# Weaving the output projection of the first attention segments into the last segment's q and k projections

## The chip, the cores and the metric

The kernel runs on one core of one Trainium2 chip. The metric is the device time of one execution in microseconds; the time given for a kernel is the median of its runs. A profiled execution shows the engines: TensorE (PE, with its weight loads as PEld), VectorE (DVE), ScalarE (ACT), GpSimd (POOL), and SyncE (SP), which issues nearly all DMAs.

## The reference

One transformer block on x of 2048 rows by 512 columns, with sa, ca, ga, sb, cb, gb the six modulation vectors of `silu(c) @ w_mod`:

```
h = layernorm(x) * (1 + ca) + sa
for s in 4 segments of 512 rows, 32 heads of 16:
    p     = softmax(q_s k_s^T / 4 + strictly-upper mask * -1e9)
    a_mem = phi(q_s) M / (phi(q_s) z + 1e-6)
    o_s   = g * a_mem + (1 - g) * (p v_s)        # g = sigmoid(beta), per head
    M, z += phi(k_s)^T v_s, sum of phi(k_s)
x = x + ga * (o @ wo)
h = layernorm(x) * (1 + cb) + sb
out = x + gb * (((h @ w_gate) * (h @ w_up)) @ w_down)
```

The mask puts −1e9 on the keys behind a query's own place (key index over query index). phi(t) is t + 1 above zero and exp(t) below.

## The kernel before, in words

All matrices that count are split into a high part and a remainder, and a product is three matmuls: high × high, remainder × high, high × remainder. A tile named `..H` is the high part (an ACT copy to a rounded type), `..L` the remainder (a subtraction on DVE or POOL).

There are two stages. The second is the gated network: for each of four segments, gate, up and down products (lines 1015 and 1036), with PE always busy. The first, in front of it, is one long loop over 32 units of four heads each (`NQ`), in which the attention of one unit is spread over several passes `v`, and everything else of the first stage is cut into small pieces and put between.

A pass has five slots. A slot emits, in this order: `q_step`, the scores of a later unit with queries in rows, on which DVE finds the maxima (two PSUM tiles, `lq0` and `lq1`, line 257); `flush()`, which emits DVE work put off in the list `later`; in slot 1 the products `tb` of the unit before (`av_step`); in slot 4 its transposes and division (`t_step`); `fill`, the pieces of other work; and `k_step`, the same scores transposed, with the exponent on ACT (line 296) and the causal select on POOL (line 299). PE's instructions keep the order in which they are written (`pe`), and so do DVE's inside the loop (`vec.eng = CV`); `pin` ties an instruction behind the last PE instruction written before it. A scheduler orders the rest by its own estimate.

`fill` takes pieces from two generators, `fa` first and then `fb`. Each yields a weight for the piece it has just emitted: 0.68 for three matmuls of 512 columns, 0.45 for four transposes. A slot with a share adds 0.25 × 5.5 to a credit, and pieces are emitted while the credit is above zero. A `yield False` ends the slot's filling at once and leaves the credit standing. `until` runs pieces without regard to credit where the next unit needs them. `weave(a, b, at)` runs generator `a` and advances `b` behind those weighted pieces of `a` whose numbers stand in `at`.

`fill_a` holds the q, k and v projections of the segments (`a_kq`, `a_v`), the first layer norm (`a_ln`), and the linear-attention memory (`a_mem`). `fill_b` holds what follows attention for segments 0 to 2: it closes the pool `pa` of the first generator and opens `bc` and `pb`; splits wo (`woH`, `woL`, line 776); loads the attention rows of a segment (`wo_load`, tiles `orl`), transposes them (`wo_op`, tiles `op`, with ACT writing `oH` at line 404 and DVE `oL`), multiplies by wo (`wo_row`, tiles `wops`, twelve matmuls for 128 rows), adds x (`wo_add`, tiles `xr`) and stores the sum; and it runs the second layer norm of segment 0 (`lnC`, transposes `ctp`, ACT `chf`) and the weight splits of the first two blocks of the gated network (`prep`). Segment 3 is done behind the loop.

PSUM tiles of all these pieces come from `bank`. Inside the loop `btag` is `["ms"]`, so there are two buffers for them.

Of the kernel before, what the change touches and what calls it, by code (L numbers as in the profile page):

```python
# [17 lines left out]
P = 128  # L18
S, D, H, DH, NSEG, L, F = 2048, 512, 32, 16, 4, 512, 1376
KT = D // P  # L20
NG = 4
# [36 lines left out]
def tile_kernel(ctx, tc, x, wq, wk_, wv, wo, beta, w_gate, w_up, w_down, c, w_mod, out):  # L58
# [82 lines left out]


    def ln(pool, hpool, xt, s, sc, sh, pfx, hb, fast):

# [33 lines left out]
        for d in range(KT):  # L178
            ps = bank(f"{pfx}tp{s}_{d}")
            for t in range(4):  # L180
                TP(ps[:, t * P:(t + 1) * P], xt[t][:, d * P:(d + 1) * P], ident)
            h = pool.tile([P, L], F32, tag="hf", name=f"{pfx}hf{s}_{d}", bufs=hb[2])
            A.activation(h, ps, AF.Identity, scale=sc[:, d:d + 1], bias=sh[:, d:d + 1])
            hi = hpool.tile([P, L], F32R, tag=hb[0].format(d), name=f"{pfx}hH{s}_{d}", bufs=hb[1])
            lo = hpool.tile([P, L], F32R, tag=hb[0].format(4 + d), name=f"{pfx}hL{s}_{d}", bufs=hb[1])
            if fast:
                V.tensor_copy(hi, h)
                V.tensor_sub(lo, h, hi.bitcast(F32))
            else:
                act.activation(hi, h, AF.Copy)  # L190
                nc.gpsimd.tensor_sub(lo, h, hi.bitcast(F32))
            hH.append(hi)
            hL.append(lo)
            yield 0.45
            if not first and d % 2 == 1:
                yield False
# [81 lines left out]
    def k_step(u, i):  # L278
# [113 lines left out]

    def wo_op(s, pb, rw, us, gs=range(NG)):

        for g in gs:
            op = bank(f"op{s}_{g}")
            for t in range(4):
                a = rw[t][:, g * P:(g + 1) * P]
                if s == NSEG - 1 and g == NG - 1:
                    a = orows[NSEG * NG - 1][:, t].rearrange("p h e -> p (h e)")  # L400
                TP(op[:, t * P:(t + 1) * P], a, ident)
            oH = pb.tile([P, L], F32R, tag="oH", name=f"oH{s}_{g}", bufs=6)
            oL = pb.tile([P, L], F32R, tag="oL", name=f"oL{s}_{g}", bufs=6)
            act.activation(oH, op, AF.Copy)
# [6 lines left out]
    def xr_load(s, pb):  # L411
        xrs = []
        for t in range(4):
            xr = pb.tile([P, D], F32, tag="xr", name=f"xr{s}_{t}", bufs=4)
            pin(nc.sync.dma_start(xr, x[rows(s, t), :]))
            xrs.append(xr)
        return xrs

    def wo_row(ps, t, us, gs):
        woH, woL = B["wo"]  # L420
        for i in gs:
            for j, (a, b) in enumerate(((us[i][0], woH), (us[i][1], woH), (us[i][0], woL))):
                MM(ps, a[:, t * P:(t + 1) * P], b[:, i, :], start=i == 0 and j == 0, stop=i == NG - 1 and j == 2)
            yield 0.68
# [4 lines left out]

    def wo_mm(s, us, pb):  # L430

        xrs = xr_load(s, pb)
        for t in range(4):
# [12 lines left out]


    papool, pa = open_pool(name="pa", bufs=2, reuse_waits="tile")
    nc.sync.dma_start(s_c, c)
# [132 lines left out]
    def load_g(nm, w, g):  # L582

        A, V = (CA if g == 0 else act), (CV if g == 0 and nm == "q" else nc.gpsimd)
        raw = staged(f"{nm}{g}")
        hi = wH[nm, g] = pa.tile([P, KT, P], F32R, name=f"w{nm}H{g}", bufs=1)
        lo = wL[nm, g] = pa.tile([P, KT, P], F32R, name=f"w{nm}L{g}", bufs=1)
        pin(nc.sync.dma_start(raw.rearrange("p (k c) -> p k c", c=P),
# [8 lines left out]
    def load_v():  # L597
        raws = []
        for k in range(KT):
            wH["v", k] = pa.tile([P, D], F32R, name=f"wvH{k}", bufs=1)  # L600
            wL["v", k] = pa.tile([P, D], F32R, name=f"wvL{k}", bufs=1)
            raws.append(staged(f"v{k}"))
# [161 lines left out]

    def wo_raw(k, pool, tag, n):
        raw = pool.tile([P, D], F32, tag=tag, name=f"wor{k}", bufs=n)
        pin(nc.sync.dma_start(raw, wo[k * P:(k + 1) * P, :]))
        nc.gpsimd.tensor_mul(raw, raw, gab)
        return raw

    def open_b():
        close(papool)
        B["bcpool"], B["bc"] = open_pool(name="bc", bufs=1, side="right", reuse_waits="tile")
        B["pbpool"], B["pb"] = open_pool(name="pb", bufs=2, reuse_waits="tile")
        pb = B["pb"]
        B["wo"] = woH, woL = [pb.tile([P, KT, D], F32R, name=n, bufs=1) for n in ("woH", "woL")]
        raws = B["raw"] + [wo_raw(k, pb, "x1", 4) for k in (2, 3)]
        yield
        for k in range(KT):
            pin(act.activation(woH[:, k, :], raws[k], AF.Copy))  # L780
            (vec if k % 2 else nc.gpsimd).tensor_sub(woL[:, k, :], raws[k], woH[:, k, :].bitcast(F32))
            yield

    def fill_a():
# [5 lines left out]
        for s in range(NSEG):  # L790
# [4 lines left out]
            for g in range(2 if s == 0 else 0, NG):  # L795
# [27 lines left out]
                if s > 0 and g == 0:  # L823
# [6 lines left out]
                    else:  # L830
                        yield from a_v(s)
                        B["orl"] = wo_load(0, wpool)
                        B["raw"] = [wo_raw(k, wpool, "wor", 2) for k in (0, 1)]
                if g == 1 and 0 < s < 3:
# [102 lines left out]
    for v in range(-2, NQ + 1):  # L937
        rate[0] = 5.5
        on, prev = 0 <= v < NQ, 0 <= v - 1 < NQ
        for slot in range(5):  # L940
# [14 lines left out]
            if v == NQ and slot == 2:  # L955
# [4 lines left out]
                us3 = []  # L960
                run(wo_op(3, B["pb"], o3, us3, range(NG - 1)))
            if prev and slot == 4:
# [19 lines left out]
    btag[:] = ["sm"]  # L982
    run(wo_op(3, B["pb"], o3, us3, (NG - 1,)))
    for t in range(4):
        run(wo_row(ps3[t], t, us3, (NG - 1,)))
        wo_add(3, t, xr3[t], ps3[t])
    close(B["pbpool"])
    close(apool)
    vec.eng = nc.vector
# [89 lines left out]
```

## Time and profile before

| | |
|---|---|
| median of 3 runs | 918.99 us (918.52 to 919.4) |
| the profiled execution | 917.64 us, of which its span 915.9 us |
| granted clock over the span | 0.989 |
| PE busy | 875.9 us, 96% |
| DVE, ACT, POOL busy | 533.5, 408.5, 316.4 us |

The profile's page gives busy times over the whole span. Windows of 5 us give them for a stretch; PE's timeline gives each instruction with the idle time before it and what ended that; the chain in order of time follows the work that ended last. A matmul of 512 columns shows as about 0.39 us on PE, but they overlap: six of them take 1.38 us in a row. PE's clock is granted by a throttle; PEclk is its share of full speed.

### The profile page before, as it was taken

Reading aid. Unit: us, or ns where it says so; the run is one execution under the profiler, and the core shown is the slowest. Engines: PE = TensorE matmul, PEld = TensorE weight load, DVE = VectorE, ACT = ScalarE, POOL = GpSimd, SP = SyncE. Lnnn points to the kernel's source line nnn. Section 1 sums busy time; section 2 is a strip of 40 time slices with the busy share of each in tenths; the row PEclk is TensorE's granted clock in tenths of the full one; section 3 lists DMA queues with packets and bytes.
Section 4 is the critical chain, followed back from the end, with each engine's and each line's share of the span. In section 5 each row is a group of like instructions: output and inputs, shape, how many; then the busy total and the mean of one; then the engine's idle time right before and its main releaser. Section 6 shows DMA issues by size and latency. Waiting matters only on the chain.

```text
span 915.9 us, 14196 instructions
## 1 busy us (share of the span) xinstructions
PE 875.9 (96%) x5084; PEld 623.0 (68%) x5084; DVE 533.5 (58%) x1587; ACT 408.5 (45%) x603; POOL 316.4 (35%) x460
## 2 busy tenths in 40 slices
PE   8998999999999899998998999999999999999998
PEld 5665656656656566565555678887888788878886
DVE  8688878888789877686886326543133213321112
ACT  3656767787577865575546412231112111211111
POOL 4545536566465752666423406540000000000000
PEclk9999999999999999999998999999999999999999
DMA  7774545664455544559651443331101110100011
GB/s 231 223 215 137 164 126 153 196 206 146 133 166 168 177 142 125 187 179 305 178 168 64 125 136 109 110 95 58 46 1 47 47 47 0 47 19 28 0 47 47
DMA packets 86215, 109.81 MB, mean 120 GB/s; under 512 B 9504, under 2 KB 58656, under 8 KB 86144
## 3 DMA queue, kind: packets, MB, share of 16 engines
q1 hardware_dynamic: 86000, 108.89, 38.6%
q8 instruction: 40, 0.66, 0.3%
q14 instruction: 31, 0.25, 0.1%
q10 hardware_dynamic: 144, 0.02, 0.0%
HBM read 67.98 MB, written 40.63 MB: 119 GB/s over the span
## 4 chain that ended last, share of the span: by engine, by line
PE 76%; DVE 14%; ACT 4%; DMA 3%; issue 1%; POOL 1%; SPq 0%; DVEq 0%; ACTq 0%; POOLq 0%
PE gps L1015 13%; PE acc L1036 13%; PE ups L1015 13%; PE tb L85 6%; DVE q L39 6%; PE k L85 6%; PE q L85 5%; PE vps L85 4%; PE wops L85 4%; PE kps L85 3%; PE qps L85 2%; ACT pt L296 1%; PE tr L88 1%; PE up L85 1%; DVE nm L39 1%
## 5 line engine op out<-in xcount | busy, mean ns | idle before, releaser
L39 DVE CUSTOM_DVE_ANT_0 q<-q,cmask 128x384 f32<-128x384 f32 (+3 forms) x512 | 246.8, 508 | 55.0 <-PE q L85 44.7
L296 ACT ACTIVATE pt<-k 128x1024 f32<-128x1024 f32 x160 | 163.7, 1023 | 75.5 <-PE k L85 72.3
L299 POOL TENSOR_SCALAR_AFFINE_SELECT pt<-pt 128x256 f32<-128x256 f32 (+1 forms) x224 | 99.5, 458 | 172.7 <-ACT pt L296 169.4
L1020 DVE TENSOR_TENSOR gs<-gs,ups 128x512 f32<-128x512 f32 (+1 forms) x44 | 30.2, 687 | 195.0 <-PE ups L1015 195.0
L85 PE MATMUL q<-kst,qst 96*128 96x384 bf16 (+3 forms) x512 | 102.1, 303 | 9.7 <-DVE nm L39 6.9
L85 PE MATMUL k<-qst,kst 98*128 98x384 bf16 (+3 forms) x512 | 98.8, 306 | 8.8 <-ACT pt L296 7.9
L1019 ACT ACTIVATE gs<-gps 128x512 f32<-128x512 f32 (+1 forms) x44 | 26.1, 597 | 146.7 <-PE gps L1015 146.7
L1023 ACT ACTIVATE mH<-gs 128x512 fp32r<-128x512 f32 (+1 forms) x44 | 27.8, 632 | 130.1 <-DVE gs L1020 126.6
L85 PE MATMUL tb<-pt,v 128*32 128x512 f32 (+3 forms) x1024 | 76.2, 437 | 1.3 <-POOL pt L299 1.3
L85 PEld LDWEIGHTS <-kst 98*128 98x128 bf16 x512 | 39.2, 100 | 51.6 <-issue 44.5
L39 DVE DVE_READ_ACCUMULATOR2_ANT nm<- 128x1 f32 x512 | 72.2, 141 | 0.0
L1015 PE MATMUL gps<-chH,gL 128*128 128x512 f32 (+1 forms) x176 | 69.3, 394 | 0.0
L1015 PE MATMUL gps<-chH,gH 128*128 128x512 f32 (+1 forms) x176 | 69.3, 394 | 0.0
L1015 PE MATMUL ups<-chH,uH 128*128 128x512 f32 (+1 forms) x176 | 69.3, 394 | 0.0
L1036 PE MATMUL acc<-dH,mL 128*128 128x512 f32 (+1 forms) x176 | 69.3, 394 | 0.0
L1036 PE MATMUL acc<-dL,mH 128*128 128x512 f32 (+1 forms) x176 | 69.2, 393 | 0.0
L1015 PE MATMUL gps<-chL,gH 128*128 128x512 f32 (+1 forms) x176 | 69.2, 393 | 0.0
L1015 PE MATMUL ups<-chL,uH 128*128 128x512 f32 (+1 forms) x176 | 69.2, 393 | 0.0
L1015 PE MATMUL ups<-chH,uL 128*128 128x512 f32 (+1 forms) x176 | 69.2, 393 | 0.0
L85 PEld LDWEIGHTS <-qst 96*128 96x128 bf16 x512 | 43.7, 98 | 36.7 <-issue 10.9
L1036 PE MATMUL acc<-dH,mH 128*128 128x512 f32 (+1 forms) x176 | 65.0, 395 | 0.0
L85 PEld LDWEIGHTS tb<-pt,v 128*32 128x32 f32 x1024 | 28.6, 110 | 40.7 <-issue 34.6
(215 smaller groups left out, 1660.5 us busy)
## 6 DMA issues: line engine op xcount, KB each, us to landing
kst<-kd SPq DMA_DIRECT2D x32, 384.0 KB, 4.6
qst<-qd SPq DMA_DIRECT2D x32, 384.0 KB, 5.3
wm<-in_w_mod_dram SPq DMA_DIRECT2D x24, 256.0 KB, 5.5
kd<-k SPq DMA_DIRECT2D x16, 384.0 KB, 3.9
qd<-q SPq DMA_DIRECT2D x16, 384.0 KB, 3.0
x<-in_x_dram SPq DMA_DIRECT2D x16, 256.0 KB, 4.1
kd<-k SPq DMA_DIRECT2D x16, 256.0 KB, 3.4
qd<-q SPq DMA_DIRECT2D x16, 256.0 KB, 3.1
```

Source lines behind the costliest of these rows:

```text
L39: i = getattr(self.eng, name)(*a, **k)
L85: return pe(nc.tensor.matmul(*a, **k))
L88: return pe(nc.tensor.transpose(*a))
L296: act.activation(pt, kp, AF.Exp, scale=0.25)
L299: sels[u, i] = nc.gpsimd.affine_select(w, w, pattern=[[0, w.shape[1]], [1, P]], compare_op=ALU.is_ge, fill=0.0, base=0, channel_multiplier=-1)
L1015: nc.tensor.matmul(ps[0:n], a[:, k, 0:n], b[k], start=j == 0, stop=j == 11)
L1019: act.activation(gs[0:n], pss[0][0:n], AF.Copy)
L1020: vec.tensor_mul(gs[0:n], gs[0:n], pss[1][0:n])
L1023: act.activation(mH[0:n], gs[0:n], AF.Copy)
L1036: nc.tensor.matmul(acc[t], a[0:n, t * P:(t + 1) * P], b[0:n, :], start=i == 0 and j == 0, stop=i == NF - 1 and j == 2)
```

## The change

Segment 0's projection, and segment 1's transposes, move from `fill_b` into the last segment's part of `fill_a`. While segment 3's second group of heads is projected (g = 1), the split of wo is woven in; with g = 2 the transposes of segment 0; with g = 3 its first rows, then the rest of them with segment 1's transposes. wo's parts now lie in the tiles of wv, and `oH` and `oL` in those of wk and wq, groups 0 and 1 for even segments and 2 and 3 for odd ones; these tiles move to a pool `pw` that stays open up to the end of the attention stage. The x rows of segment 0 come into tiles of `pa`. What is left in `fill_b` is woven anew, with segment 2's transposes and the layer norm put between the rows.

The remainder `oL` is no longer emitted with the next piece but put into `later`, so that DVE reaches it behind the maxima of the next slot. The evictions `oH` and those of the layer norms' transposes go into a list `ahead`, and the next exponent on ACT is ordered behind them. `wo_op` and the second layer norm no longer end a slot's filling, and all four subtractions of wo's split are on POOL.

```diff
@@ ln
-            A.activation(h, ps, AF.Identity, scale=sc[:, d:d + 1], bias=sh[:, d:d + 1])
+            ahead.append(A.activation(h, ps, AF.Identity, scale=sc[:, d:d + 1], bias=sh[:, d:d + 1]))
...
-            if not first and d % 2 == 1:
+            if pfx == "a" and not first and d % 2 == 1:
                 yield False
@@ k_step
-        act.activation(pt, kp, AF.Exp, scale=0.25)
+        x = act.activation(pt, kp, AF.Exp, scale=0.25)
+        while ahead:
+            tc.add_manual_dep(x.ins, ahead.pop().ins.name, NOSYNC, reason="order")
@@ wo_op
-    def wo_op(s, pb, rw, us, gs=range(NG)):
+    def wo_op(s, rw, us, gs=range(NG), stop=False):
         for g in gs:
+            flush()
             op = bank(f"op{s}_{g}")
...
-            oH = pb.tile([P, L], F32R, tag="oH", name=f"oH{s}_{g}", bufs=6)
-            oL = pb.tile([P, L], F32R, tag="oL", name=f"oL{s}_{g}", bufs=6)
-            act.activation(oH, op, AF.Copy)
+            nm = ("k", "q")[g % 2]
+            i = s % 2 * 2 + g // 2
+            oH = pw.tile([P, L], F32R, tag=f"w{nm}H{i}", name=f"oH{s}_{g}", bufs=1)
+            oL = pw.tile([P, L], F32R, tag=f"w{nm}L{i}", name=f"oL{s}_{g}", bufs=1)
+            ahead.append(act.activation(oH, op, AF.Copy))
             us.append((oH, oL))
             yield 0.45
-            pin(vec.tensor_sub(oL, op, oH.bitcast(F32)))
-            if g % 2 == 1:
+            later.append(lambda oL=oL, op=op, oH=oH: vec.tensor_sub(oL, op, oH.bitcast(F32)))
+            if stop:
+                flush()
+            if stop and g % 2 == 1:
                 yield False
@@ wo_row
         woH, woL = B["wo"]
+        flush()
@@ the split of wo
+    def wo_split():
+        woH, woL = B["wo"] = [], []
+        def raw(k):
+            r = wpool.tile([P, D], F32, tag="wor", name=f"wor{k}", bufs=2)
+            pin(nc.sync.dma_start(r, wo[k * P:(k + 1) * P, :]))
+            return r
+        raws = [raw(0), raw(1)]
+        yield
+        for k in range(KT):
+            r = raws[k]
+            nc.gpsimd.tensor_mul(r, r, gab)
+            woH.append(pw.tile([P, D], F32R, tag=f"wvH{k}", name=f"woH{k}", bufs=1))
+            woL.append(pw.tile([P, D], F32R, tag=f"wvL{k}", name=f"woL{k}", bufs=1))
+            yield
+            pin(act.activation(woH[k], r, AF.Copy))
+            nc.gpsimd.tensor_sub(woL[k], r, woH[k].bitcast(F32))
+            if k + 2 < KT:
+                raws.append(raw(k + 2))
+            yield
@@ fill_a
+                if s == NSEG - 1 and g == 1:
+                    K, Q = weave(K, ws3, (0, 1, 2, 3)), weave(Q, ws3, (0, 1, 2, 3))
+                if s == NSEG - 1 and g == 2:
+                    us0 = []
+                    op0 = wo_op(0, B["orl"], us0)
+                    K, Q = weave(K, op0, (0, 2)), weave(Q, op0, (0, 2))
                 if s == NSEG - 1 and g == NG - 1:
-                    yield from Q
+                    yield from op0
+                    B["o1"] = wo_load(1, wpool)
+                    mm0 = wo_mm(0, us0, pa, "x")
+                    yield from weave(Q, mm0, (1, 3))
                     memq.append(a_mem(s, g))
-                    yield from K
+                    yield from weave(K, mm0, (1, 3))
+                    B["us1"] = []
+                    op1 = wo_op(1, B["o1"], B["us1"])
+                    yield from weave(mm0, op1, (1, 3, 5, 7))
+                    yield from op1
                     break
@@ fill_b
-        ob = open_b()
-        next(ob)
-        o1 = wo_load(1, pb)
-        pr = prep(0, bc, pb, "cr", 3)
-        next(pr)
-        us = [[], [], []]
-        yield from weave(wo_op(0, pb, B["orl"], us[0]), ob, (0, 1, 2, 3))
-        while osegs[0] <= 2:
-            yield None
-        o2 = wo_load(2, wpool)
-        yield from weave(wo_mm(0, us[0], pb), pr, (3, 6, 9, 12))
-        yield from wo_op(1, pb, o1, us[1])
-        pr = prep(1, bc, pb, "cr", 3)
-        next(pr)
-        lg = lnC(0, pb, bc, pb, "x1", 4)
-        yield from weave(wo_mm(1, us[1], pb), lg, (1, 5, 6, 7, 8, 9, 11, 12, 13, 14))
-        B["nxt"] = yield from lg
-        yield from wo_op(2, pb, o2, us[2])
-        B["orl_free"] = True
-        yield from weave(wo_mm(2, us[2], pb), pr, (3, 6, 9, 12))
+        open_b()
+        while osegs[0] <= 2:
+            yield None
+        us2 = []
+        op2 = wo_op(2, wo_load(2, wpool), us2)
+        lg = lnC(0, pb, bc, pb, "x1", 4)
+        pr = prep(0, bc, pb, "cr", 3)
+        next(pr)
+        mm = weave(wo_mm(1, B["us1"], pb), lg, (0, 3, 4, 5, 6, 7, 8, 9, 10, 11))
+        yield from weave(weave(mm, op2, (6, 8, 10, 12)), pr, (5, 8, 10, 13))
+        yield from op2
+        B["orl_free"] = True
+        yield from pr
+        pr = prep(1, bc, pb, "cr", 3)
+        next(pr)
+        yield from weave(weave(wo_mm(2, us2, pb), lg, (1, 4, 7, 10)), pr, (5, 8, 11, 13))
+        yield from pr
+        B["nxt"] = yield from lg
```

More of the change, by code (lines that the diff above doesn't have):

```diff
@@ L139, in rows @@
         return slice(s * L + t * P, s * L + (t + 1) * P)
+    ahead = []
     def ln(pool, hpool, xt, s, sc, sh, pfx, hb, fast):
@@ L420, in wo_row @@
         woH, woL = B["wo"]
+        flush()
         for i in gs:
             for j, (a, b) in enumerate(((us[i][0], woH), (us[i][1], woH), (us[i][0], woL))):
-                MM(ps, a[:, t * P:(t + 1) * P], b[:, i, :], start=i == 0 and j == 0, stop=i == NG - 1 and j == 2)
+                MM(ps, a[:, t * P:(t + 1) * P], b[i], start=i == 0 and j == 0, stop=i == NG - 1 and j == 2)
             yield 0.68
@@ L763, in tile_kernel @@
     B = {}
[L765 to L769, printed above, removed]
+    def wo_split():
[17 more added lines that the diff above has]
+            yield
     def open_b():
@@ L774, in open_b @@
         B["pbpool"], B["pb"] = open_pool(name="pb", bufs=2, reuse_waits="tile")
[L775 to L782, printed above, removed]
     def fill_a():
@@ L832, in fill_a @@
                         B["orl"] = wo_load(0, wpool)
-                        B["raw"] = [wo_raw(k, wpool, "wor", 2) for k in (0, 1)]
+                        ws3 = wo_split()
+                        next(ws3)
                 if g == 1 and 0 < s < 3:
@@ L960, in tile_kernel @@
                 us3 = []
-                run(wo_op(3, B["pb"], o3, us3, range(NG - 1)))
+                run(wo_op(3, o3, us3, range(NG - 1), True))
             if prev and slot == 4:
@@ L982, in tile_kernel @@
     btag[:] = ["sm"]
-    run(wo_op(3, B["pb"], o3, us3, (NG - 1,)))
+    run(wo_op(3, o3, us3, (NG - 1,), True))
     for t in range(4):
```

18 lines of the change are left out of this document (10 added, 8 removed).

## The prediction

> **What bounds the kernel now.** I read the page first: busy shares, the chain, then the granted clock.
>
> ```profile
> PE 875.9 (96%) x5084; PEld 623.0 (68%) x5084; DVE 533.5 (58%) x1587; ACT 408.5 (45%) x603; POOL 316.4 (35%) x460
> PEclk9999999999999999999998999999999999999999
> PE 76%; DVE 14%; ACT 4%; DMA 3%; issue 1%; POOL 1%; SPq 0%; DVEq 0%; ACTq 0%; POOLq 0%
> ```
>
> PE carries three quarters of the chain. The change adds no matmul, so it can win only PE idle and lost clock where the output projection runs, and lose only by making new idle. Hence the second view: windows of 5 us between 360 and 540 us (after the window: its length, then busy us of PE, PEld, DVE, ACT, POOL, then PEclk). These are the windows that lose most.
>
> ```profile
> 370.00:375.00 5.00, 3.72 (x41) 1.67 (x40) 3.15 (x10) 1.44 (x3) 3.36 (x5) 1.00 0.46 136
> 420.00:425.00 5.00, 2.07 (x13) 1.24 (x12) 2.98 (x8) 3.63 (x6) 3.52 (x6) 0.99 0.67 203
> 425.00:430.00 5.00, 5.00 (x22) 3.89 (x22) 4.93 (x14) 2.77 (x4) 3.39 (x4) 0.67 1.07 352
> 435.00:440.00 5.00, 3.82 (x21) 2.34 (x19) 4.04 (x17) 2.27 (x3) 0.41 (x1) 1.00 0.81 211
> 455.00:460.00 5.00, 3.79 (x29) 2.70 (x28) 4.90 (x18) 3.79 (x6) 1.40 (x3) 1.00 0.64 176
> 485.00:490.00 5.00, 3.67 (x22) 2.45 (x22) 4.90 (x17) 2.59 (x4) 1.46 (x3) 0.97 0.14 52
> 490.00:495.00 5.00, 5.00 (x42) 2.05 (x41) 3.65 (x13) 2.50 (x4) 2.70 (x3) 0.69 0.14 52
> 495.00:500.00 5.00, 2.81 (x21) 1.84 (x19) 0.87 (x3) 4.74 (x7) 2.65 (x5) 1.00 0.01 2
> 500.00:505.00 5.00, 4.32 (x24) 3.61 (x24) 2.27 (x5) 3.72 (x7) 2.80 (x4) 0.66 0.61 211
> ```
>
> The third view, PE's timeline and the chain in order of time, says what PE waited for there (brackets: idle before, and who ended it).
>
> ```profile
> 373.31 0.64 PE L85 MATMUL tb<-pt,v 128*32 128x256 f32 x8 [1.28 <-POOL pt L299]
> 422.52 0.66 PE L88 MATMUL op<-ident,orl 128*128 128x128 f32 x4 [1.03 <-DVE oL L39]
> 424.81 1.10 PE L88 MATMUL op<-ident,orl 128*128 128x128 f32 x4 [1.64 <-DVE oL L39]
> 457.68 1.25 PE L88 MATMUL op<-ident,orl 128*128 128x128 f32 x8 [0.79 <-DVE oL L39]
> 489.57 1.01 PE L88 MATMUL ctp<-ident,x 128*128 128x128 f32 x4 [0.87 <-ACT chf L183]
> ...
> 423.45 4.82 DMA orl<-od
> 428.29 5.83 DMA xr<-in_x_dram
> 434.21 0.69 DVE xr L39
> ```
>
> Two things repeat. Transposes of the projection wait for DVE's remainder `oL`, because inside the attention loop `bank` has the two `ms` buffers alone; and at the opening of the new pools DVE stands at the add into `xr` until its load lands, with the next maxima behind it.
>
> **What can be given back.** Around the opening: 2.93 idle (420–425), 5 × (1 − 0.67) = 1.65 of clock (425–430), 1.18 idle (435–440): 5.8 us. Segment 1's transposes: 1.2 us (455–460). Layer norm and segment 2's transposes, standing in a row without other work: 1.33 + 1.55 + 2.19 + 0.68 + 1.70 = 7.5 us over the last four windows, two of these terms being clock (0.69, 0.66). The tail of the products behind a select: 1.28. Together 15.7 us, if all goes and nothing comes for it. At the opening the `xr` loads of segment 0 are now issued from `pa`, passes before their add, and each pair of transposes is spaced out, so I take it all as gone; some may stay, and 12 is the lower end.
>
> **Where the pieces land.** The order of fillers is counted, not guessed. Each of slots 0, 2, 3, 4 of a pass adds 0.25 × 5.5 = 1.375 of credit; a block of three matmuls uses 0.68, four transposes 0.45, a memory step 0.5. The count fits the trace of before: for pass 31 slot 0 it gives five blocks in one go, out of credit that `yield False` had held back, and there the chain has 15 matmuls.
>
> ```profile
> 447.06 2.29 PE tb L85 x32
> 450.32 1.38 PE wops L85 x6
> 460.48 2.29 PE tb L85 x32
> 505.16 3.70 PE wops L85 x15
> 524.04 0.45 PE op L88 x4
> ```
>
> So a block is 1.38 / 2 = 0.69 us and four transposes 0.45; a pass, from one run of `tb` to the next, is 460.48 − 447.06 = 13.4, a slot 2.7. I write pass.slot. For the changed kernel the count gives: split of wo 21.4–22.4; segment 0's transposes 23.0, 23.3, 23.4, 24.0; its rows 24.3–27.4 with segment 1's transposes at 26.2, 26.4, 27.0, 27.2; pools opened at 28.0; segment 1's rows 28.0–30.2 with the layer norm's statistics and segment 2's transposes at 28.4, 29.0, 29.2, 29.4; segment 2's rows 30.2–32.2 with the layer norm's transposes. The same three blocks as now are left to drain at 32.2: the loop gets no shorter by credit, only by less waiting. The last projections are done at 25.4, in front of their need at 27.1, so that delay is hidden.
>
> **What is added: waits for one of two banks.** A projection of k or q, or a row of wo, holds one `ms` buffer through all its blocks. With transposes woven in, the other is held until DVE has written `oL`, now emitted behind the next maxima. Where the next tile starts in that same slot, PE has issued the slot's q matmuls and must sit through the maxima and the remainder, less the PE work in front. Prices from DVE's timeline, start to next start:
>
> ```profile
> 455.05 0.69 DVE L39 CUSTOM_DVE_ANT_0 q<-q,cmask 128x512 f32<-128x512 f32 x1
> ...
> 456.31 0.25 DVE L39 RECIPROCAL rd<-tr 128x16 f32<-128x16 f32 x1
> 456.60 0.43 DVE L39 TENSOR_TENSOR orow<-tr,rd 128x256 f32<-128x256 f32 x1
> 456.94 1.28 DVE L39 TENSOR_TENSOR oL<-op,oH 128x512 fp32r<-128x512 f32 x2
> 458.14 0.56 DVE L39 CUSTOM_DVE_ANT_0 q<-q,cmask 128x384 f32<-128x384 f32 x1
> ...
> 459.91 1.28 DVE L39 TENSOR_TENSOR oL<-op,oH 128x512 fp32r<-128x512 f32 x2
> 444.11 0.68 DVE L39 TENSOR_TENSOR crd<-crd,gbb 128x512 f32<-128x512 f32 x1
> 446.49 0.68 DVE L39 TENSOR_TENSOR xr<-xr,wops 128x512 f32<-128x512 f32 x1
> 441.29 0.42 DVE L39 CAST uH<-cru 128x512 fp32r<-128x512 f32 x1
> 484.98 0.54 DVE L39 TENSOR_SCALAR x<-x,cmv,cy 128x512 f32<-128x512 f32 x1
> 471.87 0.68 DVE L39 BATCH_NORM_STATS2 cst<-x 128x6 f32<-128x512 f32 x1
> 472.68 0.66 DVE L39 BATCH_NORM_STATS2 cst<-x 128x6 f32<-128x512 f32 x1
> L404 ACT ACTIVATE oH<-op 128x512 fp32r<-128x512 f32 x16 | 9.2, 596 | 14.4 <-PE op L88 14.4
> ```
>
> Maxima of slots 2 and 4 take 456.31 − 455.05 = 1.26, those of slots 0 and 3 459.91 − 458.14 = 1.77; a remainder or an add 0.68 (or 0.64 in a pair); a statistic with its aggregate 0.81; reciprocal and rows of t_step 0.63. Then, place by place:
>
> - 23.3: q's first block needs k's bank, as the transposes hold the other: an eviction, 0.60 alone, up to 1.6 behind an exponent; I take 0.9.
> - 23.4: 1.26 + 0.68 = 1.9. 24.0: 1.77 + 0.68 − 0.69 = 1.8.
> - 26.4: the next row waits for the add of the row just ended: 1.26 + 0.68 − 0.45 = 1.5. 27.3: for segment 1's last remainder: 1.77 + 0.68 = 2.4.
> - 28.3 to 29.4, where DVE itself is full: 28.3 holds 1.77 + 2 × 0.81 + 0.68 + 0.42 = 4.5 us against a slot's 2.7, so DVE enters 29.0 about 1.8 late. 28.4 waits 0.7 of that; 29.0's transposes 1.77 + 0.68 − 0.69 + 1.1 = 2.9; the next row, whose bank comes free by an add behind a cast, a statistic and a multiply, 0.42 + 0.81 + 0.68 + 0.68 − 0.45 = 2.1; 29.4's row 1.26 + 0.63 + 0.54 + 0.68 − 0.45 = 2.7. Together 8.4.
> - 31.3, with no maxima left: 0.4.
>
> Sum 17.3 us. The lower end is 7: DVE may have finished part of it before PE arrives. The upper end is 22, with DVE late elsewhere too.
>
> **Clock.** In before the window 485–490 had PE busy for 3.67 of 5 us, with no gap over 0.87, and the next ran at 0.69. The pile at 29.0–29.4 looks like that: I take one such drop, 5 × (1 − 0.69) = 1.6, between 0 and 3.2. The Trainium skill, in "TensorE: Matmul & The Clock Gate" (section "Why this matters for your kernels"), says the clock falls back after an idle gap over about 3 us. By that rule none of these waits costs clock, and the sum would lose its 1.6; the row at 490–495 speaks against it.
>
> **What I cost at nothing.** The eight halves of wo move from the opening to 21.4–22.4: four ACT copies, four POOL multiplies and four POOL subtractions (two of these were DVE's). The rows are
>
> ```profile
> L768 POOL TENSOR_TENSOR wor<-wor,gab 128x512 f32<-128x512 f32 x2 | 2.6, 1318 | 0.3 <-DMA wor<-in_wo_dram 0.3
> L780 ACT ACTIVATE woH<-wor 128x512 fp32r<-128x512 f32 x4 | 2.5, 633 | 1.5 <-POOL wor L768 1.4
> ```
>
> Blocks of matmuls cover them; behind them on POOL stand the selects, so without cover the 1.28 at 373 us returns. Evictions pinned ahead of the exponent delay it by at most 0.6 each and spare a 0.87 as at 489.57; zero, between −1 and +2. On SP, pass 28 queues four `orl`, three weight, four `xr` and four `x` loads; the add comes three slots (8 us) after its load, against 5.83 landing time: hidden.
>
> **Sum.** 17.3 + 1.6 − 15.7 = +3.2 us on the profiled execution, 917.64 to 920.8. The runs' median lies 1.35 above that, so 922.2. Within 0.2% (1.8 us) is about what a measurement here can't tell from no change.
>
> **Rivals.** (A) Slower by more, the load wall moves to 28.0: fifteen loads of 256 KB, plus the next heads' two of 384 KB, at the 352 GB/s of 425–430 take 13 us; if SP stands behind the last write of `x1d`, `xr` lands late and the 5.8 of the old opening stays: 928. For it: 423.45 and 428.29; against: three slots of room. (B) Faster: banks cheap. DVE finishes each remainder while PE is in its blocks, so only the 7 of the lower end are paid, with no clock drop: 7 − 15.7 = −8.7, or 910.3; with half of the waits at 28.3–29.4 gone and no drop, about −2.6 to 916.4. It decides where the waits and the clock of passes 23 to 32 fall below 15.7 together. For it: DVE's share is 58% overall; against: 4.90 of 5 busy at 455–460 and 485–490, where a remainder cost PE its idle. (C) No change: the same filler, merely reordered, gives as much as it takes, 919.
>
> **Chances.** Forecast 0.44, A 0.16, B 0.29, C 0.11: faster 0.29, same 0.11, slower 0.60. The range: 911 leaves the best of B out, 929 takes A in.
>
> **What would show it.** Right: PE idle before `op` and `wops` with DVE `oL` and `xr` as releasers, near passes 23–24 and 26–29, the clock below 0.8 once after 28.4, and the windows of the old opening near full. Wrong: PE above 4.8 of 5 through those passes (B), or DVE waiting for DMA `xr` (A). The gate stage behind the loop should keep its length, as its matmuls are untouched.

## The result and the profile after

| | us, median | profiled execution | span | mean clock |
|---|---|---|---|---|
| before | 919.19 (918.52 to 919.91) | 917.64 | 915.9 | 0.989 |
| after | 953.07 (951.85 to 955.94) | 953.57 | 951.8 | 0.972 |

The changed kernel is slower: ratio 1.0384, 95% interval 1.0361 to 1.0407. The forecast had the side right and the size wrong: 922.2, with 929 as the upper end.

The page after, the lines that answer to the three of before (busy shares, granted clock in 40 slices, the chain):

```profile
PE 891.4 (94%) x5083; PEld 628.8 (66%) x5084; DVE 530.5 (56%) x1585; ACT 409.2 (43%) x603; POOL 317.9 (33%) x462
PEclk8998999999999999979998999999999999999999
PE 57%; DVE 6%; ACT 2%; POOL 2%; issue 1%; DMA 1%; SPq 0%; DVEq 0%; ACTq 0%; POOLq 0%
```

PE is busy for 15.5 us more with one matmul record less, so the same matmuls run slower; its idle grows too. Of the clock's slices before one is below 0.9, the 22nd (481 to 504 us). After, the 18th is in the sevens (405 to 428), the 22nd again below 0.9 (500 to 523), and so are the first and the fourth, in the start. The chain's shares of this page add up to 69% only, so they are not set against those of before.

The place of the loss is one stretch. From run 20 of `tb` to run 32 (343.72 to 519.42 before, 346.56 to 555.45 after) it takes 175.7 us before and 208.9 after, +33.2; behind it, the gate stage and the end take 396.5 and 396.4. The profiled executions differ by 35.9; the other 2.8 lie ahead of the stretch, where in the first 120 us 7.5 us of clock are lost against 3.3. Pass by pass, in us:

```
before  13.2 13.2 15.7 13.5 13.7 19.3 14.7 13.4 15.3 16.5 17.0 10.2
after   13.2 13.2 16.5 26.8 20.8 13.0 19.0 21.0 21.2 20.2 12.4 11.6
```

Over that stretch, from windows of 2.5 us, PE's idle (length less busy) goes from 13.8 to 34.8, and the clock lost (busy × (1 − granted clock)) from 4.2 to 15.2: 21.0 + 11.0 of the 33.2. Who ended the idle says the list of PE's waits in the stretch (us in total, times, longest), first its main lines before, then after:

```profile
PE op L88 <- DVE oL L39: 3.5, 3, 1.6
PE q L85 <- DVE nm L39: 3.0, 6, 0.7
PE k L85 <- ACT pt L296: 2.1, 4, 1.0
```

```profile
PE op L88 <- DVE oL L39: 18.1, 9, 3.8
PE wops L85 <- DVE xr L39: 5.8, 4, 2.3
PE wops L85 <- DVE oL L39: 2.8, 1, 2.8
PE tb L85 <- POOL pt L303: 2.6, 2, 1.3
```

Nine sets of transposes, all but the first of each of three segments, wait for the remainder of the set before. The windows of 5 us after (length; busy of PE, PEld, DVE, ACT, POOL; granted clock; DMA share; GB/s) where most is lost:

```profile
375.00:380.00 5.00, 2.63 (x20) 1.47 (x21) 2.59 (x6) 3.08 (x6) 5.00 (x6) 1.00 0.33 111
395.00:400.00 5.00, 2.02 (x15) 1.15 (x15) 4.11 (x16) 1.81 (x3) 2.07 (x4) 1.00 0.50 159
400.00:405.00 5.00, 4.31 (x15) 2.29 (x14) 0.01 (x1) 2.88 (x5) 1.75 (x3) 0.55 0.21 79
405.00:410.00 5.00, 3.45 (x13) 2.29 (x12) 2.55 (x7) 1.18 (x2) 1.45 (x3) 0.50 0.39 133
410.00:415.00 5.00, 3.31 (x18) 2.20 (x18) 2.40 (x9) 1.36 (x2) 0.63 (x1) 0.84 0.49 150
500.00:505.00 5.00, 2.54 (x14) 1.34 (x12) 4.83 (x19) 1.55 (x2) 3.08 (x3) 1.00 0.14 52
505.00:510.00 5.00, 3.14 (x9) 1.87 (x10) 2.86 (x7) 1.74 (x4) 3.90 (x7) 0.63 0.49 157
520.00:525.00 5.00, 2.60 (x18) 1.70 (x17) 4.90 (x16) 1.03 (x1) 1.53 (x4) 1.00 0.02 3
525.00:530.00 5.00, 4.61 (x20) 3.16 (x18) 2.54 (x10) 1.62 (x2) 0.63 (x1) 0.67 0.69 198
```

The pass of 26.8 us shows the loop that makes it. Lines from PE's timeline after, the last two from later passes, then from DVE's:

```profile
386.65 0.61 PE L88 MATMUL op<-ident,orl 128*128 128x128 f32 x4
...
396.24 0.61 PE L85 MATMUL q<-kst,qst 96*128 96x384 bf16 x4
399.62 0.66 PE L88 MATMUL op<-ident,orl 128*128 128x128 f32 x4 [2.77 <-DVE oL L39]
...
407.79 1.09 PE L88 MATMUL op<-ident,orl 128*128 128x128 f32 x4 [1.55 <-DVE oL L39]
...
413.80 0.82 PE L88 MATMUL op<-ident,orl 128*128 128x128 f32 x4 [1.69 <-DVE oL L39]
...
427.30 0.50 PE L85 MATMUL wops<-woH,oH 128*128 128x512 f32 x1 [2.84 <-DVE oL L39]
...
506.84 1.09 PE L88 MATMUL op<-ident,orl 128*128 128x128 f32 x4 [3.85 <-DVE oL L39]
```

```profile
396.67 0.57 DVE L39 CUSTOM_DVE_ANT_0 q<-q,cmask 128x384 f32<-128x384 f32 x1
...
398.94 0.63 DVE L39 TENSOR_TENSOR oL<-op,oH 128x512 fp32r<-128x512 f32 x1
404.99 0.70 DVE L39 CUSTOM_DVE_ANT_0 q<-q,cmask 128x512 f32<-128x512 f32 x1 [5.42 <-PE q L85]
```

The transposes of 386.65 get their remainder at 398.94, three slots later. At 396.8 PE has issued the slot's scores and stands until DVE has been through that slot's maxima (from 396.67) and the remainder (at 398.94). Then DVE stands for 5.42 us, because the scores of the next slot are behind the transposes, a k and a q block on PE, and these run at half clock. Each engine waits for the other in turn; neither is full.

### The profile page after: what moved, and what is told of

Read it like the earlier page. It is cut to its first block, busy times and chain, and to the rows that moved or that the text cites. A ratio compares the mean times of both kernels' runs of the same rounds, so it can differ in the third digit from the quotient of the medians.

```text
span 951.8 us, 14195 instructions
## 1 busy us (share of the span) xinstructions
PE 891.4 (94%) x5083; PEld 628.8 (66%) x5084; DVE 530.5 (56%) x1585; ACT 409.2 (43%) x603; POOL 317.9 (33%) x462
## 4 chain that ended last, share of the span: by engine, by line
PE 57%; DVE 6%; ACT 2%; POOL 2%; issue 1%; DMA 1%; SPq 0%; DVEq 0%; ACTq 0%; POOLq 0%
PE gps L1048 13%; PE acc L1069 13%; PE ups L1048 13%; PE wops L85 4%; PE k L85 3%; PE tb L85 3%; DVE q L39 3%; PE q L85 2%; PE vps L85 1%; PE qps L85 1%; PE kps L85 1%; DMA wor<-in_wo_dram 1%; PE op L88 1%; DVE oL L39 1%; ACT pt L298 1%
## 5 line engine op out<-in xcount | busy, mean ns | idle before, releaser
L298 ACT ACTIVATE pt<-k 128x1024 f32<-128x1024 f32 x160 | 163.7, 1023 | 80.2 <-PE k L85 77.2
L85 PE MATMUL k<-qst,kst 98*128 98x384 bf16 (+3 forms) x512 | 101.4, 312 | 8.1 <-ACT pt L298 7.7
```

Source lines behind the costliest of these rows:

```text
L85: return pe(nc.tensor.matmul(*a, **k))
L298: x = act.activation(pt, kp, AF.Exp, scale=0.25)
```

## The experiments

Each ran beside the kernel before on the same chip, whose median was 918.3 to 920.0 in the five sets. Stretch, idle and clock are those of each kernel's profiled execution, as above.

| kernel | median | ratio, 95% interval | stretch | PE idle | clock lost |
|---|---|---|---|---|---|
| before | 919.19 | | 175.7 | 13.8 | 4.2 |
| after | 953.07 | 1.0384 (1.0361–1.0407) | 208.9 | 34.8 | 15.2 |
| append first | 934.74 | 1.0174 (1.0142–1.0206) | 187.9 | 23.8 | 6.8 |
| remainder at once | 924.46 | 1.0079 (1.0053–1.0105) | 180.2 | 18.7 | 3.8 |
| before, evictions first | 924.04 | 1.0051 (1.0031–1.0072) | 176.4 | 14.5 | 4.6 |
| evict to SBUF | 922.62 | 1.0023 (1.0001–1.0044) | 173.0 | 11.9 | 4.3 |
| xr loads first | 923.11 | 1.0035 (1.0012–1.0058) | 174.0 | 12.9 | 3.9 |
| and wo early | 918.33 | 0.9985 (0.9963–1.0007) | 170.2 | 11.0 | 2.8 |
| before, evict to SBUF | 926.89 | 1.0083 (1.0057–1.0109) | 180.3 | 16.7 | 5.6 |
| xr in other memory | 918.47 | 0.9993 (0.9970–1.0017) | 167.2 | 8.9 | 1.7 |
| statistics later | 913.92 | 0.9944 (0.9921–0.9967) | 163.9 | 6.8 | 0.0 |
| mended, remainder on DVE | 917.32 | 0.9983 (0.9964–1.0002) | 170.8 | 10.2 | 3.4 |
| mended, remainder behind | 949.89 | 1.0329 (1.0291–1.0367) | 203.5 | 31.3 | 14.5 |
| last segment on DVE | 909.74 | 0.9891 (0.9865–0.9916) | 166.1 | 6.3 | 3.0 |
| no order of evictions | 907.61 | 0.9870 (0.9842–0.9898) | 163.7 | 6.7 | 0.0 |
| order behind only | 907.08 | 0.9867 (0.9837–0.9897) | 164.7 | 7.5 | 0.0 |

### When the remainder is emitted

In `wo_op` the remainder is put on the list behind the `yield`, so not before its generator is resumed, and that is when the next transposes are due, up to three slots later. `flush()` at their head then emits it behind that slot's maxima. The first edit puts it on the list ahead of the `yield`, so that the next slot's `flush()` takes it:

```diff
+            later.append(lambda oL=oL, op=op, oH=oH: vec.tensor_sub(oL, op, oH.bitcast(F32)))
             yield 0.45
-            later.append(lambda oL=oL, op=op, oH=oH: vec.tensor_sub(oL, op, oH.bitcast(F32)))
```

> The changed kernel with one line moved: the remainder goes into the list before the generator yields, so the next slot's flush emits it; in the changed kernel it goes there only when the generator is resumed, which is right in front of the next transposes. Theory 1 (the place of emission makes the waits): PE's waits for oL in front of op fall from 18.1 us to 5 to 8, the lost clock of passes 20 to 32 from 15.2 to 5 to 9, and the time from 953 to 925 to 934. Theory 2 (two banks are too few wherever the remainder is emitted): waits in front of op stay above 13 us and the time above 944. The prediction had read the code as if it were this kernel, so its sum of 922.2 is tested here.

The second emits it on the spot:

```diff
+            vec.tensor_sub(oL, op, oH.bitcast(F32))
             yield 0.45
-            later.append(lambda oL=oL, op=op, oH=oH: vec.tensor_sub(oL, op, oH.bitcast(F32)))
```

> The changed kernel with the remainder emitted at once, in front of the yield and of the next maxima, instead of through the list. Theory 1: the bank is free a slot earlier still, but DVE stands at each remainder until ACT has evicted, about 1 us for each of twelve with the maxima behind it: waits for oL in front of op under 5 us, PE waits for maxima (nm) up by 3 to 6, time 922 to 935. Theory 2: 944 or more.

PE's waits between 340 and 535 us, first with the append ahead, then with the remainder at once:

```profile
PE wops L85 <- DVE xr L39: 6.5, 3, 3.0
PE op L88 <- DVE oL L39: 5.0, 3, 1.8
PE op L88 <- DVE xr L39: 3.7, 1, 3.7
PE wops L85 <- DVE oL L39: 2.4, 1, 2.4
```

```profile
PE wops L85 <- DVE oL L39: 6.0, 4, 2.2
PE op L88 <- DVE xr L39: 5.5, 1, 5.5
```

One line moved takes 13 of the 18.1 us of that wait and 8.4 of clock, 18.3 us of the median; at once takes 10 more, and PE's waits for maxima, which were expected to rise by 3 to 6, stay at 0.2. What is left with the list is mostly another wait, rows and an `op` behind DVE's add `xr` (6.5 and 3.7); at once, it is one `op` behind that add (5.5) and four rows whose first matmul waits for a remainder that it doesn't read, so for the bank (6.0). The first of the two kernels is the one that the prediction had in mind, and it comes out at 934.74, not at 922.2; the section on the prediction takes that up.

### The order of evictions alone

The kernel before with the list `ahead`, and without the `yield False` of `wo_op` and the second layer norm:

```diff
+        x = act.activation(pt, kp, AF.Exp, scale=0.25)
+        while ahead:
+            tc.add_manual_dep(x.ins, ahead.pop().ins.name, NOSYNC, reason="order")
```

> The kernel before with two parts of the change alone: evictions of transposes ordered in front of the next exponent, and no end of the slot's filling after every second group of transposes of the projection and the second layer norm. If these are harmless as I costed them: 916 to 922, with the 0.87 and 1.5 us waits for chf gone. If they are part of the loss (an exponent delayed by each of the evictions): 925 or more, with PE's waits for pt up.

It is 0.5% slower, some 4.6 us, between the two outcomes expected, but the stretch only 0.7 longer; waits `op` for `oL` there went up to 6.9 us in 5. Run 20 of `tb` comes 4.9 us later, and 3.3 of these are clock lost ahead of the stretch. More on that at the end.

### The bank's second reader

Both ACT (`oH`) and DVE (`oL`) read the bank, so it is held until the later one. Here ACT copies it to SBUF, and the split is made from the copy, its remainder on POOL:

```diff
-            ahead.append(act.activation(oH, op, AF.Copy))
+            of = wpool.tile([P, D], F32, tag="wor", name=f"of{s}_{g}", bufs=2)
+            ahead.append(act.activation(of, op, AF.Copy))
+            act.activation(oH, of, AF.Copy)
+            nc.gpsimd.tensor_sub(oL, of, oH.bitcast(F32))
...
-            later.append(lambda oL=oL, op=op, oH=oH: vec.tensor_sub(oL, op, oH.bitcast(F32)))
```

> The changed kernel, with ACT copying the transposes to SBUF in full, and high part (ACT) and remainder (POOL) made from that copy, so that a bank comes free with one ACT copy and DVE has no remainder. Theories 1 and 2 both say: waits for oL in front of op 18.1 to about 0, PE idle of passes 20 to 32 from 34.8 to 12 to 18, lost clock from 15.2 to under 7, time 917 to 930. Theory 3 (the loss is in the new order itself: DVE full near pass 28, wo's loads on POOL, the add behind xr): above 938. The waits for the add into xr, 5.8 us, should stay in part under all three.

The transposes' waits for `oL` in the stretch are gone, and it is 2.7 us shorter than before's. Two passes are still long, 16.6 and 23.4 us. In the second, PE, DVE and SP have one long wait each (from the lists of their waits):

```profile
PE op L88 <- DVE xr L39: 6.5, 1, 6.5
DVE cst L39 <- DMA x<-x1d: 5.9, 1, 5.9
SPq L424 <- DMA x1d<-xr: 4.0, 1, 4.0
```

SP stands at segment 1's `xr` loads until the write of segment 0's last rows to `x1d` has landed, and behind them are the loads of the weights and of `x1d`; DVE stands at the layer norm's first statistic for that last load, with the add that releases PE's bank behind it. This is the load wall of rival A.

To ask whether the two parts of the change are needed for this gain, the kernel before got the same eviction alone (`of` from the same buffers):

> The kernel before in its own order, with the eviction path alone changed: ACT copies op to SBUF and rounds oH from there, POOL makes oL. If the bank's release is all that the new order needed, and the order itself gives back nothing, this gains as much as the two others: waits op<-oL of 3.5 us go and the time is 913 to 916. If what the new order gives back is its own (opening, row of transposes without work beside them): only 1 to 4 us come, 915.5 to 918, and windows 420-425 and 485-505 keep their idle.

It lost 0.8%. With before's burst of transposes at the opening, two copies per tile stand on ACT beside wo's split. From 340 to 535 us PE waits 4.1 us for `of`, once for 3.1, and rows wait for POOL (two of the seven behind the loop); the last line is from ACT's timeline at the opening:

```profile
PE wops L85 <- POOL oL L407: 4.2, 7, 1.5
PE op L88 <- ACT of L405: 4.1, 3, 3.1
423.76 1.08 ACT L405 ACTIVATE of<-op 128x512 f32<-128x512 f32 x2 [1.61 <-DVE woL L39]
```

The last line shows that a part of this is the edit's own: `of` lies in the two tiles `wor` of wo's split, so the first copy waits 1.61 us until DVE has made `woL` from one of them. Segment 2's transposes and rows come in a burst without a split, and their pass takes 20.9 us against 17.0, with 2.3 us of waits for POOL's `oL` in it. So the copy didn't pay without the new order; whether it would with tiles of its own is not shown.

### The two long passes

First guess, on the kernel with the copy to SBUF: issue the `xr` loads in front of all others.

```diff
+        xr1 = xr_load(1, pb)
         op2 = wo_op(2, wo_load(2, wpool), us2)
...
```

> The eviction path of the run before (ACT copies the transposes out, DVE has no remainder), and segment 1's four xr loads issued first behind the opening of the new pools, ahead of the other loads in SP's queue and in the memory released earliest. If the 6.5 us wait at one op and the pass of 23.5 us come from that load queue (rival A): that pass falls to 14 to 16 us, DVE's wait for x<-x1d of 5.9 goes under 2, and the time is 912 to 917, below the kernel before. If they come from DVE being full in that pass (forecast's reading): the pass stays above 20 us and the time within 919 to 924.

No gain; that pass takes 24.0. DVE isn't full in it, though: it stands 6.8 us in front of `x<-x1d`. It fits that tiles which come first in the new pool lie on those that came first in the old one, the `x` tiles, and these hold the rows of segment 0 until they are written. On top of this, wo's loads were moved ahead of the v projections:

```diff
-                        yield from a_v(s)
-                        B["orl"] = wo_load(0, wpool)
                         ws3 = wo_split()
                         next(ws3)
+                        B["orl"] = wo_load(0, wpool)
+                        yield from a_v(s)
```

> The run beside it, and wo_load(0) with the first two loads of wo emitted ahead of the v projections, so that POOL's multiplies need not wait for their DMA. If the 16.5 us of pass 22 to 23 come from POOL standing at its multiply with the selects behind it: that pass falls to 13.5 us, POOL's wait of 3.7 us for wor goes, and the time is 2 to 3 us under the run beside it (910 to 914). If they come from the split's work itself on POOL (4 multiplies of 1.32 us and 4 subtractions): the pass stays at 15.5 or more and the time within 1 us of the run beside it.

Pass 22 to 23 falls from 16.8 to 13.6, the stretch by 3.8 and the median by 4.8, which still misses 910 to 914, since the other long pass stays at 23.8. POOL's timeline with the `xr` loads first, then with wo early as well:

```profile
372.01 2.52 POOL L789 TENSOR_TENSOR wor<-wor,gab 128x512 f32<-128x512 f32 x2 [2.27 <-DMA wor<-in_wo_dram]
374.49 0.63 POOL L303 TENSOR_SCALAR_AFFINE_SELECT pt<-pt 128x512 f32<-128x512 f32 x1
```

```profile
371.80 0.63 POOL L303 TENSOR_SCALAR_AFFINE_SELECT pt<-pt 128x512 f32<-128x512 f32 x1 [0.62 <-ACT pt L298]
372.40 1.27 POOL L789 TENSOR_TENSOR wor<-wor,gab 128x512 f32<-128x512 f32 x1
```

In the first the multiplies wait 2.27 us for their loads, and a select stands behind both until 374.49; in the second two parts are done by then and the select comes at 371.80.

Then the tiles for `x1d` were placed first, on the old `x` tiles, and `xr` behind them:

```diff
+        x1 = [pb.tile([P, D], F32, tag="x1", name=f"x1_0_{t}", bufs=4) for t in range(4)]
         xr1 = xr_load(1, pb)
...
-        lg = lnC(0, pb, bc, pb, "x1", 4)
+        lg = lnC(0, pb, bc, pb, "x1", 4, x1)
```

> The run with loads and wo early, with one thing changed: the four tiles for x1d (which wait for those writes anyway) are placed first in the new pool, on the memory of the old x tiles, so that segment 1's xr tiles lie elsewhere and SP need not wait for the write of segment 0's last row. If that wait of 4.2 us on SP, with all later loads behind it, makes the pass of 23.8 us: the wait goes, the pass falls to 18 to 20 us (the statistic then waits 1 to 2 us for its load's 5.4 instead of 6.1), and the time is 912 to 915. If the loads would be late regardless, because x<-x1d has to follow the same write: SP's wait only moves to that load, and pass and time stay within 1 us.

and, with that, the layer norm's statistics three blocks later:

```diff
-        mm = weave(..., lg, (0, 3, 4, 5, 6, 7, 8, 9, 10, 11))
+        mm = weave(..., lg, (0, 6, 7, 8, 9, 10, 11, 12, 13, 14))
```

> The same, and the layer norm's four statistics three blocks (4 us) later in segment 1's products, so that DVE does not reach the first of them before its load lands. If DVE's place in front of a load that has not landed is the cause: the wait of DVE for x<-x1d goes under 2 us, no wait of PE over 2.5 us is left in that pass, it takes 14 to 16 us, and the time is 908 to 912, below the kernel before by about 1%. If DVE is full there in any case: PE's idle before op only moves one pass on and the time stays above 916.

SP's wait of 4.2 us goes with the first; the pass falls to 20.8 (18 to 20 expected), the stretch by 3.0, but the median not at all; its profiled execution loses 2.8 us of clock behind the loop, where the run it starts from loses none. DVE's wait is shorter, not gone; it goes with the second (DVE's and PE's waits with `xr` in other memory, then PE's longest with the statistics later):

```profile
DVE cst L39 <- DMA x<-x1d: 4.1, 1, 4.1
PE op L88 <- DVE xr L39: 4.6, 1, 4.6
```

```profile
PE q L85 <- DVE nm L39: 3.1, 6, 1.1
```

That version is faster than the kernel before, by 0.6%, with no clock lost in the stretch. Its median missed what was expected (908 to 912) by 2 us, and a part of the reason is behind the loop: from the last `tb` run the six kernels so far with the copy take 399.1 to 401.6 us, those without it 396.4 to 396.5; this one takes 400.8, with PE waiting 2.6 us for POOL's `oL` and 1.7 us of clock lost there, where segment 3's transposes go through the same copy. So that segment was put back on DVE:

```diff
+            if stop:
+                ahead.append(act.activation(oH, op, AF.Copy))
+            else:
                 of = wpool.tile(...)
...
             yield 0.45
+            if stop:
+                vec.tensor_sub(oL, op, oH.bitcast(F32))
```

> The run with statistics later (ACT copies out, POOL makes oL) for segments 0 to 2; segment 3's transposes, behind the loop, round oH straight from the bank and leave oL to DVE as in the kernel before. There the copy path showed 2.6 us of PE waiting for POOL oL in 40 us behind the loop, against 0.2 for DVE oL before, and one clock drop of 1.7. If those are the path's own price: the stretch behind the last tb goes from 400.8 back to 396.5, and the time is 909 to 911.5. If that stretch is longer for another reason: within 1 us of the run with statistics later (914).

The end takes 396.5 again, and the median is 909.74.

### How much is the remainder alone

Two kernels with all mends of "statistics later" but the remainder on DVE: emitted at once, and as the change has it.

> The run with statistics later, but with the remainder on DVE, emitted at once behind its transposes (two readers of the bank, ACT and DVE). If DVE's release of the bank is still a cost of its own: waits op<-oL and wops<-oL of 5 to 8 us come back and it is 6 to 10 us above that run (915 to 920). If the loads were all of it: within 2 us of that run.

> All mends of the run with statistics later, but the remainder as in the changed kernel: appended when its generator is resumed, on DVE behind the maxima. If this one edit causes most of the loss: nine waits op<-oL of 13 to 18 us come back, with 4 to 10 us of clock, and the time is 935 to 947. If the waits were mostly the loads' and the split's, and the remainder only the last in a queue of causes: 920 to 930.

917.32 and 949.89: the place of this one instruction is worth 32.6 us, nearly the whole of the change's loss, and with it in place the other mends together give 3 us. At once, rows wait 6.6 us for `oL` and no `op` does; it costs 3.4 us over the copy (913.92), where 6 to 10 were expected, and 6.9 in the stretch, as the copy loses some 4 behind the loop. Behind is worse by 3 us than the 935 to 947 expected. The wait that fills the second (PE, the whole stretch):

```profile
PE op L88 <- DVE oL L39: 17.5, 9, 2.8
```

### The order of evictions again

Of the kernel with the last segment on DVE, two versions: the list emptied without a dependence, and the order dropped for the first layer norm only.

```diff
-        while ahead:
-            tc.add_manual_dep(x.ins, ahead.pop().ins.name, NOSYNC, reason="order")
+        ahead.clear()
```

> The run with segment 3 on DVE, and no order between evictions and exponents at all (the list is emptied without a dependence). In the kernel before with that order alone the median rose by about 4.6 us, the stretch of the projection by 0.7 only, so the rest lay in the first stage before it. If the order costs that: run 20 of tb comes at 343 to 344 instead of 346.9 and the time is 905 to 908. If run 20 comes late for another reason (clock in the first 120 us, differing from execution to execution): within 1 us of 909.7. If the weave needs the order, its evictions come late and waits for op or of of over 3 us appear in the stretch: 911 or more.

> The same, with the order kept for the projection's transposes and the second layer norm and dropped for the first layer norm alone. If the first layer norm's evictions pinned ahead of the exponents are what costs: 905 to 908, at or below the run without any order. If the order costs nothing there: 909 to 911.

Both reach 907, 2 to 3 us below in the medians, with intervals that overlap the 0.9891 of the kernel they start from. Run 20 of `tb` comes at 344.21 without any order and at 346.43 with the part kept; the difference is clock lost in the first 120 us (3.2 and 6.3 us), which varies between executions of other kernels too. The order is not needed and costs little; how much, and through which evictions, stays open.

## Why the prediction was wrong, by its own steps

**Waits for one of two banks: right mechanism, 17.3 against 27.3 us.** PE's idle in front of `op` and `wops` with DVE `oL` or `xr` as releasers is 18.1 + 5.8 + 2.8, and 0.6 of an `op` behind `xr`. Place by place, in order of time, forecast and measured: 23.3 0.9 and 2.77; 23.4 1.9 and 1.55; 24.0 1.8 and 1.69; 26.4 1.5 and 2.01; 27.3 2.4 and 2.34; 28.4 to 29.4 8.4 and 8.8; 31.3 0.4 and 0.8. Four were not in the list at all: the first row at 24.3 (2.84), the transposes at 27.0 and 27.2 (1.14, 1.12) and a row at 28.0 (2.34). That the priced places are near is partly luck: at 23.3, 26.4 and 27.3 another wait stands there than the one that was priced (a remainder for an eviction, a remainder for an add, an add for a remainder).

This is the step that failed, a reading of code: I took each remainder as emitted behind the maxima of the next slot, but it enters the list only when the generator is resumed. With the append ahead of the `yield`, the kernel is the one that I had read, and the step holds: the same waits are 5.0 + 6.5 + 3.7 + 2.4 = 17.6 us, and 26.4 (a row behind the add, 1.62) and 27.3 (a row behind `oL`, 2.43) have the size and the releaser that were priced. The misreading is worth 18.3 us of the 30.9 by which the forecast missed. The other 12.5 are there in that kernel too (934.74 against 922.2): in its profiled execution some 5.9 us of clock in the stretch, 3.2 of idle that wasn't given back, and 4.4 ahead of the stretch. So a second step failed.

**Clock: 1.6 forecast, 15.2 lost.** This is the second step. I took one drop, at 29.0 to 29.4, and its upper end was two. The waits come in rows, though, and each pile of them costs the next windows: 0.55, 0.50 and 0.84 from 400 to 415, 0.63 from 505, 0.67 from 525. By my sum the clock lost in the stretch should have fallen by 3.3 us; it rose by 11.0, a miss of 14.3, as large as that of the whole idle (6.5 forecast, 21.0 measured). In the kernel with the append ahead, where the waits are as priced, 6.8 us are lost where the sum left 0.9.

**What can be given back: 15.7, 12 as the lower end.** Only in part in the changed kernel: outside the waits above 7.5 us of idle are left (34.8 − 27.3), where the forecast left 3.0 (13.8 − 10.8). With the mends it comes: the stretch is 11.8 us shorter (175.7 to 163.9), at the lower end, with no clock lost and 6.8 us of idle left. In the opening's place the wall of loads had to be taken out by hand.

**wo's split at nothing.** Wrong as the text's own condition had it: in the changed kernel POOL is busy for 5.00 of 375 to 380, `tb` waits 2.6 for selects, and pass 22 to 23 takes 16.5 (15.7 before, where the 1.28 lies in it). What cost was not the eight operations, which are all still there with wo early, but the multiplies' wait for loads that were issued too late: 3 us of that pass.

**SP's loads hidden.** True of the changed kernel, but only because it was late for other reasons: SP stands 1.1 us for the write of `x1d`, and DVE never for `x<-x1d`. With the remainder out of the way rival A's wall stands at 28.0, though not for bandwidth but for a write that had to land before the tile could be used again, and a statistic in front of the load: DVE waits 3.2 us there with the append ahead, 5.0 with the remainder at once and 5.9 with the copy, where it was 6.5 us of PE.

**Evictions ahead at nothing.** In the kernel before, the order and the freed `yield False` cost 4.6 us in the median, where the upper end was 2; in the mended one its removal gives 2 to 3, with intervals that overlap. In the kernel before most of it lies ahead of the stretch, 3.3 us as clock; the cause stays open.

**Right:** the gate stage kept its length (396.5 and 396.4); the side; DVE's `oL` and `xr` as the releasers. Rival B's "remainder done while PE is in its blocks" is not what the change becomes with the remainder at once: no `op` then waits for `oL`, but rows do, and the kernel takes 924.46, not 910 to 916.

In sum for the stretch: forecast +3.2 (idle 17.3 − 10.8, clock 1.6 − 4.9, the 15.7 split into its idle and its clock), measured +33.2 (idle +21.0, clock +11.0). The range was too narrow by its own ends: 22 of waits, 3.2 of clock and 12 given back make +13.2, or 932.

## What to carry to other kernels

In a generator, work put off behind a `yield` is put off until somebody resumes it, and where the pieces are woven with others, that is when the buffer is wanted; put it on the list ahead of the `yield`, or emit it at once, or let the engine that reads first copy the bank out, so that nobody else holds it. With two buffers and in-order engines, price a weave by who releases each buffer and in which slot, then add the clock of each pile of waits. A load that waits for a buffer's last write stalls every load behind it: place such tiles where only loads that wait for that write anyway will fall (3.0 us of the stretch here, nothing in the median by itself).

## What the runs showed of the hardware

The clock falls without a long gap. From 396 to 400 us after PE is busy for 0.85 and 0.38 of 2 us each, its longest gap 2.77; the next window of 2 us is granted 0.61, and the two behind it run at half clock (windows of the changed kernel):

```profile
396.00:398.00 2.00, 0.85 (x7) 0.36 (x5) 1.61 (x8) 1.02 (x1) 0.72 (x2) 1.00 0.22 38
398.00:400.00 2.00, 0.38 (x3) 0.38 (x4) 1.50 (x7) 0.00 (x0) 0.94 (x2) 1.00 0.54 180
400.00:402.00 2.00, 1.31 (x7) 0.54 (x5) 0.00 (x0) 1.22 (x3) 0.16 (x1) 0.61 0.34 131
402.00:404.00 2.00, 2.00 (x6) 1.21 (x7) 0.00 (x0) 0.73 (x2) 1.16 (x1) 0.50 0.19 66
404.00:406.00 2.00, 2.00 (x9) 1.19 (x7) 1.01 (x3) 1.52 (x2) 1.43 (x2) 0.50 0.29 98
```

The Trainium skill, in "TensorE: Matmul & The Clock Gate" (section "Why this matters for your kernels"), ties the fall to idle gaps of over about 3 us. By that rule one gap of this stretch would count, the 3.85 at 506.84; here the measurement decides, with most drops behind shorter gaps. The Trainium skill, in the same page's section "A second HAM failure mode: psum-queue depth-cycling", says that brief, frequent idling between groups of matmuls makes the clock swing. With that the trace agrees: nine waits of 1.1 to 3.9 us in front of `op`, and 15.2 us of clock lost among them.

Nor does the share of busy time settle it. The same place with the statistics later, then with the last segment on DVE:

```profile
465.00:470.00 5.00, 3.65 (x24) 2.50 (x22) 3.25 (x12) 2.64 (x4) 3.57 (x5) 1.00 0.95 330
470.00:475.00 5.00, 4.31 (x43) 2.00 (x43) 4.90 (x12) 2.96 (x5) 5.00 (x6) 1.00 0.39 114
```

```profile
465.00:470.00 5.00, 3.21 (x18) 2.14 (x17) 3.32 (x12) 2.21 (x3) 3.40 (x5) 0.92 0.73 264
470.00:475.00 5.00, 4.31 (x16) 1.97 (x18) 4.90 (x12) 2.36 (x4) 4.60 (x5) 0.50 0.39 111
```

These two differ by 0.44 us of idle, and over the stretch the one loses 3.0 us of clock where the other loses none. Over the kernels of the table clock lost goes up with idle, from 0.0 at 6.7 us to 15.2 at 34.8: half a us for each us from end to end (15.2 / 28.1), but not evenly (3.8 at 18.7, 4.2 at 13.8), and near the lower end 0.0 at 6.8 and 3.0 at 6.3 look like chance.
